# Linear attention and MLP on one NeuronCore: another start-up for batch 0 (one load for its last v, kv copied out by one engine, fill matmuls that begin later) and another tie rule in the planner

## The chip, the cores and the metric

The kernel runs on one NeuronCore of a Trainium2 chip. The metric is the device time of one execution in microseconds (us), the median of three runs. The profile is of one further execution. Short names of the engines: PE is TensorE (PEld its weight loads), DVE is VectorE, ACT is ScalarE, POOL is GpSimd, SP is SyncE.

## The reference

The inputs are q, k and v, each 8 batches x 8 heads x 576 rows x 64, in float32.

```python
kv  = einsum('bhsd,bhse->bhde', k, v)           # 64 x 64 per head, over all 576 rows
o   = einsum('bhsd,bhde->bhse', q, kv)
x   = o / sqrt(mean(o*o, -1) + 1e-6) * g_norm   # then the heads side by side: (8, 576, 512)
xn  = (x - mean(x)) / sqrt(var(x) + 1e-6) * g_ln
out = x + relu(xn @ w_ch1) @ w_ch2              # 512 -> 2048 -> 512
```

## The kernel before

**Tiles.** The 8 x 576 rows of x make 36 tiles of 128 rows: four tiles per batch ("slots" 0 to 3) and one tile for the last 64 rows of two batches together (slot 4). Tiles 0 to 3 are batch 0, tiles 4 to 7 batch 1, tile 8 their slot 4, then batch 2, and so on. Four tiles make a block.

**Per batch.** POOL loads k, v and q by DMA with a cast to bf16. `k_permute` puts k in the order of the matmul, `kv_mm` (L446) makes kv of two heads at a time in PSUM, and `kv_out` (L459 and L461) copies its two diagonal parts, `upper` false and true, into `kv_pack`. q has to be turned to `qT`: `q_turn_pe` (L410) does it on PE with the identity, and `q_turn_out` (L390, L392) copies it out of PSUM; `q_turn_dma` (L431) does it by a DMA on SP's queue. Batch 0's slots 0 to 3 and batch 1's slots 0 and 1 are turned on PE, all else by DMA. Batch 1's q comes in one load to `qb` and is put in order by four ACT copies; batch 2's comes to the same `qb` in the same way, with two copies.

**Per tile.** `t_out` (L469) makes o; ACT squares it (L482), DVE reduces (L491) and multiplies by g_norm (L486), ACT takes the root (L495), DVE inverts and scales (L500, L517), takes the mean, and makes `xc` (L543). `xc` is turned to `xT`, on PE for tiles 0 to 11 (L550, copied out by ACT, L557), by DMA on SP's queue after that (L561). The first MLP matmul is `m1` (L600 tile by tile in blocks 0 and 1, groups of 16 matmuls with 128 moving columns; L615 in later blocks, 4 matmuls of 512), with relu on ACT (L607, L622). The second is `m2` (L634, groups of 4), and DVE adds x (L641). SP stores.

**Order.** Every piece of work is registered with `add(engine, occupation, duration, key, dependencies, function)`. `run_plan` is a list scheduler that runs while the program is built: it takes at each step the instruction that could start earliest by its own cost figures, with the lower key first where several are ready, and the program is written in the order of the planned starts. So each engine has a fixed order of instructions, and the cost figures in `add` do nothing on the chip but set this order. Main MLP groups follow one list with a window of `LOOK = 8`.

**The start.** POOL issues batch 0's k in two halves of the heads, v in a half (heads 0 to 3) and two quarters (heads 4, 5 and 6, 7), q of slot 0 in two halves, then slots 1 to 3 between the four quarters of `w1`, then `w2` and batch 1. Tile 0 is worked in two halves (`HALVED`), and tiles 0 and 1 have `xc` turned in two halves (`HALF_TURN`). `idle_mm` puts fill matmuls that nobody reads into PE's stream, from 1.3 us planned time on (`WARM_FROM`), on a zeroed tile `blank`; before `kv_mm` they are as many as fit the planned gaps, later 0.6 of the gap. They come in packs of 12, 24, 13, 10 and 18. `kv_out` of batch 0 has DVE copy the lower part and ACT the upper, each waiting for `kv_mm` alone:

```python
        for u in (0, 1):
            eng, cost = (("DVE", dve_cost), ("ACT", act_cost))[u]
            ab.append(add(eng, *cost(64 * (h1 - h0) // 2), -59 + i, [s, z0], ...
```

**Later loads.** For batches from 3 on, `gate` puts a small POOL copy that reads a tile's `xT` ahead of the loads of k, q and v, so that they wait for tiles f-8, f-7 and f-6, where f is the batch's first tile (for batch 3 tiles 5, 6, 7).

Of the kernel before, what the change touches and what calls it, by code (L numbers as in the profile page):

```python
# [14 lines left out]
def kernel(  # L15
# [11 lines left out]
    nc = tc.nc  # L27
# [21 lines left out]
    XB = 18  # L49
    NEAR = 0.35  # L50
    BANKS = {"mm": 4, "out": 2, "kvt": 2}
    WARM_FROM = 1.3
    HALVED = (0,)
    SPLIT_STORE = (25,)
    HALF_TURN = (0, 1)
    PARTS = ((0, 4), (4, 8))

# [47 lines left out]
    def run_plan():  # L107
        free = dict.fromkeys(("PE", "ACT", "DVE", "POOL", "SP"), 0.0)
        free["POOL"], free["SP"], free["DVE"], free["ACT"] = 1.2, 0.7, 0.8, 2.1
        lanes = {"POOL": [], "SP": []}  # L110
        server = 3.7
        left = {e: [s for s in steps if s.eng == e] for e in free}
        mains = [s for s in steps if s.main]
        order = []

        def ready(s):
            r = 0.0
            if s.behind and s.behind.start is None:
                return None
            for d in s.deps:  # L120
                if d.done is None:
                    return None
                r = max(r, d.done + (s.lag if d.dma else 0.0))
            if s.dma and len(lanes[s.eng]) >= 8:
                r = max(r, lanes[s.eng][-8].done)
            if s.alloc and len(slots[s.alloc]) >= BANKS[s.alloc]:
                f = slots[s.alloc][-BANKS[s.alloc]].frees
                if f.done is None:
                    return None
                r = max(r, f.done)  # L130
            return r + 0.06

        while any(left.values()):
            window = set()
            for s in mains[:LOOK]:
                if (s.key < 16) != (mains[0].key < 16) or 16 <= mains[0].key < 32 and window:
                    break
                window.add(id(s))
            best = None
            for e, ls in left.items():  # L140
                cand = []
                for s in ls:
                    if s.main and id(s) not in window:
                        continue
                    r = ready(s)
                    if r is not None:
                        cand.append((max(r, free[e]), s.key, s))
                    if e == "POOL":
                        break
                if not cand:  # L150
                    continue
                t = min(c[0] for c in cand)
                near = [c for c in cand if c[0] <= t + 1e-6]
                c = min(near, key=lambda c: c[1])
                while e in ("DVE", "ACT", "PE"):

                    near = [d for d in cand if d[0] <= t + NEAR and d[1] < c[1] - 0.7
                            and c[0] + c[2].occ > d[0] + 0.1 and (e != "PE" or d[1] < -3)]
                    if not near:
                        break  # L160
                    c = min(near, key=lambda d: d[:2])
                t, s = c[0], c[2]
                if best is None or t < best[0]:
                    best = (t, s)
            assert best is not None, "the plan is stuck"
            t, s = best
            s.start = t
            free[s.eng] = t + s.occ
            if s.dma:
                lanes[s.eng].append(s)  # L170
                lat, wk, tail = s.dma
                begin = max(server, t + s.occ + lat)
                server = begin + wk
                s.done = begin + wk + tail
            else:
                s.done = t + s.dur
            if s.alloc:
                slots[s.alloc].append(s)
            left[s.eng].remove(s)
            if s.main:  # L180
                mains.remove(s)
            order.append(s)
        order.sort(key=lambda s: s.start)
        return order
# [14 lines left out]
        return s  # L199


    blank = consts.tile([128, 128], bf16, name="blank")
    nc.vector.memset(blank, 0.0)
    eps_attn = consts.tile([128, 1], f32, name="eps_attn")
    nc.vector.memset(eps_attn, EPS_ATTN)
    eps_ln = consts.tile([128, 1], f32, name="eps_ln")
# [80 lines left out]
    for i, (k_, n, c) in enumerate(groups):  # L287
# [17 lines left out]
    rate6, rate4, rate1 = 400.0, 395.0, 305.0  # L305

    load = {}
    row = [add("SP", 0.4, 1.4, -99, [], lambda x=x, f=f: nc.sync.dma_start(
        scales[:, f], bass.AP(tensor=x.tensor, offset=x.offset,
                              ap=[[x.shape[0], 1], list(x.ap[0])])))  # L310
        for x, f in ((moe_g_ln, slice(0, Dm)), (g_norm, slice(Dm, Dm + D)))]
# [48 lines left out]
    pool_load(("v", 0, 0), load_kv(vb, v, 0, 0, 4), rate6)  # L360
    pool_load(("k", 0, 4), load_kv(kb, k, 0, 4, 8), rate6)
    pool_load(("q", 0, 0, 0), load_slot(qp[0], q, 0, 0, 0, 4), rate1)
    pool_load(("v", 0, 4), load_kv(vb, v, 0, 4, 6), rate6)
    pool_load(("v", 0, 6), load_kv(vb, v, 0, 6, 8), rate6)
    pool_load(("q", 0, 0, 4), load_slot(qp[0], q, 0, 0, 4, 8), rate1)
    ident = pool_do(0.6, identity_fn)
    pool_load(("q", 0, 1), load_slot(qp[0], q, 0, 1), rate1)
# [281 lines left out]


    k0p = []
    for i, (h0, h1) in enumerate(PARTS):
        k0p.append(add("DVE", 0.13 * (h1 - h0) + 0.07, 0.13 * (h1 - h0) + 0.15, -80 + i, load["k", 0, h0],
                       lambda h0=h0, h1=h1: k_permute(nc.vector, 0, h0, h1)))
    for h0, h1 in PARTS:
        add_q_turn_pe(0, 0, load["q", 0, 0, h0], -57 + h0 / 4, ("DVE", "ACT")[h0 // 4], h0, h1)
    for t in (1, 2, 3):
        add_q_turn_pe(0, t, load["q", 0, t], (-4.5, pos[2] - 9, pos[3] - 9)[t - 1],
                      ("ACT", "ACT", "DVE")[t - 1])
    kvs = []  # L660

    urgent = []
    for i, (h0, h1) in enumerate(((0, 4), (4, 6), (6, 8))):
        hps = range(h0 // 2, h1 // 2)
        w = (h1 - h0) / 8
        s = add("PE", 1.36 * w, 1.36 * w + 0.25, -60 + i, load["v", 0, h0] + [k0p[h0 // 4]],
                lambda hps=hps, i=i: kv_mm(0, hps), alloc="kvt")
        ab = [s]
        for u in (0, 1):
            eng, cost = (("DVE", dve_cost), ("ACT", act_cost))[u]  # L670
            ab.append(add(eng, *cost(64 * (h1 - h0) // 2), -59 + i, [s, z0],
                          lambda h0=h0, h1=h1, u=u: kv_out(
                              0, h0 // 2, h1 // 2, (nc.vector, nc.scalar)[u], u == 1)))
        s.frees = ab[-1]
        kvs.append(ab[1:])
        if i == 0:
            kv_first = s
        else:
            urgent.append(s)
        kv_mm_done = s  # L680
    adone[0]["kvmm"] = kv_mm_done
    kvs[1:] = [kvs[1] + kvs[2]]
    adone[0]["kv"] = kvs[0] + kvs[1]
    load_w_kv1()
    pool_load(("q", 0, 4), load_fifth(qp[0][:, 4, :, :], q, 0), 180.0, [])
    pool_load(("q", 1, 4), load_fifth(qp[1][:, 4, :, :], q, 1), 180.0, [])
# [97 lines left out]
    def plan_tile(n):  # L784
# [8 lines left out]
            deps.append(main_at(okey[n] - EARLY))  # L793
        def cost(c, h0, h1):
            return c((h1 - h0) * D)
        halves = PARTS if n in HALVED else ((0, H),)

        q0 = okey[n] if n // 4 not in FINE else p - 12
        xs = []
        for h0, h1 in halves:  # L800
            hh = dict(h0=h0, h1=h1)
            w = (h1 - h0) / H
            q0 = p - 12 if n // 4 in FINE else okey[n]
            d = kvs[len(xs)] + [adone[0]["qT", 0][len(xs)]] if n in HALVED else deps
            o = add("PE", 0.23 * len(bs) * w, 0.23 * len(bs) * w + 0.2, okey[n], d,
                    lambda hh=hh: t_out(n, **hh), alloc="out")
            if n in HALVED:
                urgent.append(o)
            sq = add("ACT", *cost(act_cost, h0, h1), q0 + 4,
                     [o] + [done[n - 3]["red"] if n >= 3 else None], lambda hh=hh: t_sq(n, **hh))  # L810
            red = add("DVE", 0.6 * w, 0.6 * w + 0.08, q0 + 5, [sq], lambda hh=hh: t_red(n, **hh))
# [14 lines left out]
        mean = add("DVE", 0.15 if few else 0.8, 0.2 if few else 0.9, q0 + 7.5, xs, lambda: t_mean(n))  # L826
        m1_before = blk[m - 3]["m1done"] if m >= 3 else None
        turned = []
        for h0, h1 in ((0, 4), (4, 8)) if n in HALF_TURN else halves:
            ff = dict(f0=h0 * D, f1=h1 * D)  # L830
            w = (h1 - h0) / H
            xc = add("DVE", 0.6 * w + 0.06, 0.6 * w + 0.15, q0 + 8, [mean, load["gl"][0]],
                     lambda ff=ff: t_xc(n, **ff))
            if n < N_PE_TURN:
                tp = add("PE", 0.23 * w, 0.23 * w + 0.22, q0 + 8.2, [xc, ident, m1_before],
                         lambda ff=ff: t_turn_pe(n, **ff), alloc="kvt")
                if n in HALVED:
                    urgent.append(tp)
                tp.frees = add("ACT", *cost(act_cost, h0, h1), q0 + 8.5, [tp],
                               lambda ff=ff: t_turn_out(n, **ff))  # L840
                turned.append(tp.frees)
            else:
# [7 lines left out]
        if m in FINE or i == 3:  # L850
            vd = var if m in FINE else blk[m]["var"]
            e = last_pos[n if m in FINE else 4 * m] - 6
            if few:
                vd = [add("DVE", 0.33, 0.4, e, vd, lambda: b_var(n))]
            s = add("ACT", 0.2, 0.3, e + 1, vd, lambda: b_std(n))
            r = add("DVE", 0.12, 0.2, e + 2, [s], lambda: b_rstd(n))
            for j in ((n,) if m in FINE else range(4 * m, 4 * m + 4)):
# [85 lines left out]
    def idle_mm(count):  # L943
        if "idle" not in blk[0]:
            blk[0]["idle"] = psum.tile([128, 512], f32, tag="mm", name="idle_ps", bufs=BANKS["mm"])
        for _ in range(count):
            nc.tensor.matmul(blk[0]["idle"][:, 0:128], lhsT=blank, rhs=blank, start=True, stop=True)

    order = run_plan()
    first_mm = min(s.start for s in order if s.main)  # L950
    pe_end, idle = WARM_FROM, {}
    for s in order:
        if s.eng != "PE":
            continue
        if s.start <= first_mm:
            gap = s.start - pe_end
            if s.start <= kv_first.start:
                idle[id(s)] = int(gap / 0.107 + 0.5)
            elif gap > 0.3 and not s.main and (s not in urgent or gap > 1.2):
                idle[id(s)] = int(0.6 * gap / 0.056)  # L960
        pe_end = s.start + s.occ
    for s in order:
        if id(s) in idle:
# [31 lines left out]
```

## Time and profile before

| | |
|---|---|
| median of 3 runs | 294.14 us (294.11 to 294.18) |
| profiled execution, its own time | 294.14 us |
| its span in the profile | 292.4 us |
| PE busy | 284.2 us, 97% of the span |
| DVE, ACT, POOL busy | 164.4, 143.4, 65.9 us |
| granted PE clock, all 40 slices | 9 (90% of full speed or more) |
| DMA | 35.73 MB; 188 to 205 GB/s from 5 to 60 us |
| first row of m1 matmuls (L600) | 16.52 us |
| start of the last PE stretch, L634 x96 | 275.02 us |

The span is counted from the first to the last profiled instruction; the execution's own time holds 1.74 us beside it. In a row of the timeline, equal instructions in a row are merged: "4.71 2.74 PE ... x24" is 24 instructions from 4.71 us on, of which the last ended 2.74 us later. A matmul ends about 0.2 us after it was issued, while the next is already running, so the rate is read from the starts.

### The profile page before, as it was taken

How to read it: one execution, taken by the hardware profiler on the slowest of the kernel's cores; microseconds unless marked ns; L12 is line 12 of the kernel's file. 1: busy time of each engine (PE TensorE's matmuls, PEld its weight loads, DVE VectorE, ACT ScalarE, POOL GpSimd, SP SyncE). 2: the span in 40 equal slices, each digit the busy share in tenths (PEclk: the TensorE clock that was granted, in tenths of full speed). 3: DMA queues.
4: the chain of work that ended last, by engine and by line, in shares of the span. 5: the costliest groups of instructions: out<-in, count | busy, mean ns of one | idle time of the engine just before them, and what ended most of it. 6: DMA issues, size and time to landing. Idle time of an engine off the chain costs nothing.

```text
span 292.4 us, 5167 instructions
## 1 busy us (share of the span) xinstructions
PE 284.2 (97%) x2049; PEld 161.3 (55%) x2049; DVE 164.4 (56%) x357; ACT 143.4 (49%) x292; POOL 65.9 (23%) x93
## 2 busy tenths in 40 slices
PE   8869999999999999999999999999999999999995
PEld 6759945976745445444544445444544444444444
DVE  1597048468883997557655775477557755320022
ACT  3469954887846612761276127611761177017400
POOL 8983320105506405404050406000000000000000
PEclk9999999999999999999999999999999999999999
DMA  7999999943998997993999399932101310120012
GB/s 96 186 199 205 204 198 178 252 73 70 173 171 136 158 183 161 174 203 77 188 103 161 98 181 119 168 81 91 56 18 54 92 54 18 57 86 22 0 74 72
DMA packets 109116, 35.73 MB, mean 122 GB/s; under 512 B 87715, under 2 KB 104739, under 8 KB 109092
## 3 DMA queue, kind: packets, MB, share of 16 engines
q0 software_dynamic: 72624, 18.35, 64.8%
q1 hardware_dynamic: 36228, 16.92, 25.2%
q8 instruction: 16, 0.26, 0.4%
q10 hardware_dynamic: 240, 0.13, 0.2%
q14 instruction: 8, 0.07, 0.1%
HBM read 36.70 MB, written 9.44 MB: 158 GB/s over the span
## 4 chain that ended last, share of the span: by engine, by line
PE 83%; DMA 9%; POOL 6%; issue 0%; ACT 0%; DVE 0%; POOLq 0%
PE mm_ps L634 41%; PE mm_ps L615 33%; DMA qb<-in_q_dram 7%; PE mm_ps L600 4%; PE out_ps L469 3%; PE kv_ps L446 2%; DMA qT<-qp 2%; POOL qp L262 1%; POOL w L342 1%; POOL vb L241 1%; POOL kb L241 1%; PE xT_ps L550 1%; POOL w L344 0%; ACT qp L390 0%; PE qT_ps L410 0%
## 5 line engine op out<-in xcount | busy, mean ns | idle before, releaser
L634 PE MATMUL mm_ps<-w,m 128*128 128x512 bf16 (+2 forms) x608 | 129.5, 368 | 0.0
L615 PE MATMUL mm_ps<-xT,w 128*128 128x512 bf16 x448 | 100.6, 379 | 0.0
L622 ACT ACTIVATE m<-mm_ps 128x512 bf16<-128x512 f32 x112 | 66.8, 597 | 50.3 <-PE mm_ps L615 49.4
L634 PEld LDWEIGHTS <-m 128*128 128x128 bf16 x608 | 57.2, 98 | 60.8
L615 PEld LDWEIGHTS <-w 128*128 128x128 bf16 x448 | 43.1, 98 | 48.8
L491 DVE TENSOR_REDUCE ss<-sq 128x8 f32<-128x512 f32 (+1 forms) x37 | 24.8, 669 | 49.3 <-ACT sq L482 49.3
L641 DVE SCALAR_TENSOR_TENSOR x<-mm_ps,rstd,x 128x512 f32<-128x512 f32 (+2 forms) x38 | 27.3, 720 | 41.8 <-PE mm_ps L634 41.7
L482 ACT ACTIVATE sq<-out_ps 128x512 f32<-128x512 f32 (+1 forms) x37 | 21.6, 583 | 38.4 <-PE out_ps L469 38.3
L600 PE MATMUL mm_ps<-xT,w 128*128 128x128 bf16 x512 | 31.0, 219 | 1.2 <-DMA w<-in_moe_w_ch_dram 0.7
L600 PEld LDWEIGHTS <-w 128*128 128x128 bf16 x512 | 29.3, 98 | 2.5 <-issue 0.9
L543 DVE SCALAR_TENSOR_TENSOR xc<-x,mv,gl 128x512 bf16<-128x512 f32 (+1 forms) x38 | 27.2, 724 | 1.2
L486 DVE TENSOR_TENSOR xg<-out_ps,gn 128x512 f32<-128x512 f32 (+1 forms) x37 | 24.7, 668 | 0.2
L607 ACT ACTIVATE m<-mm_ps 128x512 bf16<-128x512 f32 x32 | 18.5, 597 | 3.2 <-PE mm_ps L600 2.9
L721 POOL COPY mark<-xT 128x1 bf16<-128x1 bf16 x15 | 6.3, 422 | 54.5 <-DMA xT<-xc 52.1
L495 ACT ACTIVATE rms<-ss,eps_attn 128x8 f32<-128x8 f32 (+1 forms) x37 | 11.1, 299 | 12.3 <-DVE ss L491 12.2
L521 DVE TENSOR_TENSOR x<-xg,inv 128x512 f32<-128x512 f32 x24 | 16.6, 691 | 0.8
L537 DVE BATCH_NORM_STATS2 stats<-x 128x6 f32<-128x512 f32 x24 | 16.6, 690 | 0.5
L469 PE MATMUL out_ps<-kv_pack,qT 128*128 128x128 bf16 x160 | 14.5, 219 | 1.3 <-ACT qT L390 0.7
L469 PEld LDWEIGHTS <-qT 128*128 128x128 bf16 x160 | 11.3, 98 | 8.1 <-ACT qT L390 1.1
L446 PEld LDWEIGHTS <-kp 128*128 128x128 bf16 (+1 forms) x168 | 10.6, 101 | 1.9 <-issue 0.3
L446 PE MATMUL kv_ps<-vb,kp 128*128 128x128 bf16 (+1 forms) x144 | 11.3, 226 | 0.2
L557 ACT COPY xT<-xT_ps 128x512 bf16<-128x512 bf16 (+1 forms) x14 | 7.3, 522 | 8.1 <-PE xT_ps L550 8.1
(63 smaller groups left out, 175.2 us busy)
## 6 DMA issues: line engine op xcount, KB each, us to landing
out_dram<-x SPq DMA_DIRECT2D x31, 256.0 KB, 2.3
w<-in_moe_w_ch_dram POOLq DMA_DIRECT2D x8, 512.0 KB, 12.0
vb<-in_v_dram POOLq DMA_DIRECT2D x6, 512.0 KB, 10.9
kp<-in_k_dram POOLq DMA_DIRECT2D x5, 512.0 KB, 8.5
qp<-in_q_dram POOLq DMA_DIRECT2D x5, 512.0 KB, 9.6
qb<-in_q_dram POOLq DMA_DIRECT2D x2, 512.0 KB, 19.1
out_dram<-x SPq DMA_DIRECT2D x8, 128.0 KB, 2.7
qp<-in_q_dram POOLq DMA_DIRECT2D x10, 64.0 KB, 8.7
```

What stands on the lines that cost most here:

```text
L446: nc.tensor.matmul(ps[:, hp, :], lhsT=kp[b % 2][p, t, 2 * hp:2 * hp + 2, :].rearrange("p h d -> p (h d)"), rhs=(v5[b % 2][:, 2 * hp:2 * hp ...
L469: nc.tensor.matmul(o3[:, hp, :], lhsT=att[b]["qT"][:, 4 * t + hp, :], rhs=kv_pack[b % 3][:, hp, :], start=(i == 0), stop=(i == len(bs) - 1))
L482: nc.scalar.activation(sq[:, h0:h1, :], st[n]["ps", h0][:, h0:h1, :], func=AF.Square)
L486: nc.vector.tensor_mul(xg[:, h0:h1, :], st[n]["ps", h0][:, h0:h1, :], gn.to_broadcast([128, h1 - h0, D]))
L491: nc.vector.tensor_reduce(ss[:, h0:h1, :], st[n]["sq"][:, h0:h1, :], axis=AX.X, op=ALU.add)
L543: nc.vector.scalar_tensor_tensor(xc[:, f0:f1], in0=st[n]["x"][:, f0:f1], scalar=blk[m]["mv"][:, i, 0:1], in1=gl[:, f0:f1], op0=ALU.subtrac ...
L600: nc.tensor.matmul(ps[:, d, :], lhsT=w1[c][:, kk, d * 128:(d + 1) * 128], rhs=blk[m]["xT"][:, kk, i * 128:(i + 1) * 128], start=(kk == 0), ...
L607: nc.scalar.activation(st[n]["m1"][:, c, :, :], st[n]["m1ps", c], func=AF.Relu)
L615: nc.tensor.matmul(ps, lhsT=w1[c][:, kk, d * 128:(d + 1) * 128], rhs=blk[m]["xT"][:, kk, :], start=(kk == 0), stop=(kk == nKm - 1))
L622: nc.scalar.activation(blk[m]["m1", c][:, d, :], blk[m]["m1ps", g], func=AF.Relu)
L634: nc.tensor.matmul(st[n]["m2ps", f0], lhsT=m1_piece(n, c, d), rhs=w2[c][:, d, f0:f1], start=(c == 0 and d == 0), stop=(c == 3 and d == 3))
L641: nc.vector.scalar_tensor_tensor(x[:, f0:f1], in0=st[n]["m2ps", f0], scalar=blk[m]["rstd"][:, i, :], in1=x[:, f0:f1], op0=ALU.mult, op1=AL ...
```

## The change

- v of batch 0, heads 4 to 7: one load in place of two; its `kv_mm` is one step of 12 matmuls in place of two of 6.
- `kv_out` of batch 0: both parts on DVE, one after the other.
- `blank` and the fill matmuls from 1.3 us on go. Fill matmuls read `identity` and stand in the last 9 us of planned time before the first m1 group, with 0.8 of the planned gap. They come in packs of 9, 6, 2, 6, 17, 20, 3 and 10.
- `HALF_TURN` goes: tile 1's `xc` and `xT` are made in one piece. Slot 2's q is copied out by DVE, not ACT.
- The scheduler: only DVE and ACT may take a step with a lower key that is up to 0.35 us later, by a simpler rule; some keys and cost figures differ, and its model of DMA starts at 0 us, not 3.7.

```diff
-    WARM_FROM = 1.3
+    WARM_FROM = 9.0
...
-    HALF_TURN = (0, 1)
-    PARTS = ((0, 4), (4, 8))
...
-        server = 3.7
+        server = 0.0
...
+                if e in ("DVE", "ACT"):
+                    k0 = min(c[1] for c in near)
+                    near += [c for c in cand if c[0] <= t + NEAR and c[1] < k0 - 0.7]
                 c = min(near, key=lambda c: c[1])
-                while e in ("DVE", "ACT", "PE"):
-
-                    near = [d for d in cand if d[0] <= t + NEAR and d[1] < c[1] - 0.7
-                            and c[0] + c[2].occ > d[0] + 0.1 and (e != "PE" or d[1] < -3)]
...
-    pool_load(("v", 0, 4), load_kv(vb, v, 0, 4, 6), rate6)
-    pool_load(("v", 0, 6), load_kv(vb, v, 0, 6, 8), rate6)
+    pool_load(("v", 0, 4), load_kv(vb, v, 0, 4, 8), rate6)
...
-    for i, (h0, h1) in enumerate(((0, 4), (4, 6), (6, 8))):
+    for i, (h0, h1) in enumerate(((0, 4), (4, 8))):
         hps = range(h0 // 2, h1 // 2)
-        w = (h1 - h0) / 8
-        s = add("PE", 1.36 * w, 1.36 * w + 0.25, -60 + i, load["v", 0, h0] + [k0p[h0 // 4]],
+        s = add("PE", 0.7, 0.95, -60 + i, load["v", 0, h0] + [k0p[i]],
                 lambda hps=hps, i=i: kv_mm(0, hps), alloc="kvt")
         ab = [s]
         for u in (0, 1):
-            eng, cost = (("DVE", dve_cost), ("ACT", act_cost))[u]
-            ab.append(add(eng, *cost(64 * (h1 - h0) // 2), -59 + i, [s, z0],
-                          lambda h0=h0, h1=h1, u=u: kv_out(
-                              0, h0 // 2, h1 // 2, (nc.vector, nc.scalar)[u], u == 1)))
+            ab.append(add("DVE", 0.22, 0.26, -59 + i, [ab[-1], z0],
+                          lambda h0=h0, h1=h1, u=u: kv_out(0, h0 // 2, h1 // 2, nc.vector, u == 1)))
...
-        for h0, h1 in ((0, 4), (4, 8)) if n in HALF_TURN else halves:
+        for h0, h1 in halves:
...
-            nc.tensor.matmul(blk[0]["idle"][:, 0:128], lhsT=blank, rhs=blank, start=True, stop=True)
+            nc.tensor.matmul(blk[0]["idle"][:, 0:128], lhsT=identity, rhs=identity, start=True, stop=True)
```

The built programs show what this does to the order. On PE, with a pair of numbers for tile and quarter of `w1`, the m1 groups of tiles 0 and 1 stand:

```
before: (0,0) (0,1) (1,0) (1,1) (0,2) (1,2) (0,3) (1,3)
after:  (0,0) (0,1) (1,0) (0,2) (1,1) (0,3) (1,2) (1,3)
```

Other shifts on PE: batch 1's `kv_mm` stands before the first m2 group, not behind it; batch 1's two q turns and first two `t_out` stand together; ahead of batch 2's first `t_out`, the turn of one tile's `xc` (four matmuls) now stands behind it. POOL has the same order but for the one load less; the gates and the DMA turns of q are the same in both programs, and on SP two of the later turns of q move ahead of one turn of an `xT`.

## The prediction

> **What bounds the kernel now.** I read the page first (PE busy 97% of the span, granted clock 9 in all 40 slices), then PE's waits, the chain, the timeline of the start and the table by stretches.
>
> PE's waits, whole:
>
> ```profile
> PE idle_ps L947 <- DVE eps_ln L207: 1.0, 1, 1.0
> PE out_ps L469 <- ACT qT L390: 0.7, 2, 0.5
> PE mm_ps L600 <- DMA w<-in_moe_w_ch_dram: 0.7, 1, 0.7
> PE xT_ps L550 <- DVE xc L543: 0.6, 1, 0.6
> PE out_ps L469 <- DMA qT<-qp: 0.6, 1, 0.6
> PE mm_ps L600 <- ACT xT L557: 0.3, 1, 0.3
> PE qT_ps L410 <- DMA qp<-in_q_dram: 0.3, 1, 0.3
> ```
>
> After the start, PE waits only for a quarter of `w1` (18.99 us), for tile 1's `xT` (20.63) and for batch 2's `qT` (69.03). From 69.03 us to the end it waits for nothing. What the change costs is what PE has left to do when the last such wait ends.
>
> The chain, where it is not PE:
>
> ```profile
> 19.23 19.13 DMA qb<-in_q_dram
> ...
> 38.38 0.63 ACT qp L390
> ...
> 62.45 6.54 DMA qT<-qp
> ...
> 69.03 0.62 PE out_ps L469 x8
> ```
>
> The marks at which PE is held are landings of DMAs. The change moves no DMA but one, so I ask at each mark how late PE may come.
>
> The timeline of the start:
>
> ```profile
> 4.71 2.74 PE L947 MATMUL idle_ps<-blank 128*128 128x128 bf16 x24
> ...
> 7.56 1.44 PE L446 MATMUL kv_ps<-vb,kp 96*128 96x128 bf16 x12
> ...
> 8.79 1.43 PE L947 MATMUL idle_ps<-blank 128*128 128x128 bf16 x13
> ...
> 12.25 0.28 PE L469 MATMUL out_ps<-kv_pack,qT 128*128 128x128 bf16 x2 [0.52 <-ACT qT L390]
> ...
> 12.59 0.72 PE L947 MATMUL idle_ps<-blank 128*128 128x128 bf16 x10
> ...
> 18.99 1.07 PE L600 MATMUL mm_ps<-xT,w 128*128 128x128 bf16 x16 [0.68 <-DMA w<-in_moe_w_ch_dram]
> ```
>
> Between starts, 128 columns take 0.107 us in the first packs and 0.056 in the pack at 12.59. The starts inside the pack at 8.79 change over at 9.9 us, so full rate came 5.2 us after the gapless stretch began at 4.71, though the granted clock reads 1.00 throughout.
>
> The table by stretches:
>
> ```profile
> 5.00:10.00 5.00, 4.89 (x49) 4.73 (x47) 1.22 (x4) 0.35 (x2) 4.92 (x8) 1.00 1.39 188
> 20.00:40.00 20.00, 19.75 (x294) 16.97 (x291) 8.53 (x29) 17.25 (x38) 6.66 (x10) 1.00 1.29 205
> ```
>
> The last column is GB/s: loads run at 188 to 205 from 5 us on, one after another.
>
> **The change part by part.**
>
> *One load less.* POOL's two quarter loads take 1.28 us (row "4.20 1.28 ... x2"); one takes about 0.64. All later issues come 0.64 us earlier, the bytes are the same. Bounds: 0, if the transfers set the landings, and -0.64 if the issues do. I take 0, for at 205 GB/s the queue has no holes for an earlier issue to fill.
>
> *kv and the fills.* Here the order of the built program is walked with durations of the trace, at the slow 0.107 us first. v's first half lands as before: 12 `kv_mm` from 7.56 to 8.84, nine fills to 9.80, two q turns, six fills to 10.65. The first `t_out` needs four DVE copies in a row (kv 0.28, k 0.54, q 0.29, kv 0.28) and stands near 10.8; two fills to 11.2; 12 `kv_mm` in place of 2 x 6, to 12.5; their two copies, 0.28 each and both now on DVE, to 13.2. PE has turns and fills until 13.57, then tile 0's second `t_out`. Before it stood at 12.25, so this is +1.3 us. From there to the `xT` turn took 3.3 us before (12.25 to 15.55), so the turn comes by 16.9, two ACT copies later m1 begins at 17.7 to 17.9 (last part before: 17.15), and ends after 16 x 0.056 = 0.9 at 18.6 to 18.8. The cover is the next group's wait for `w1`, which ended at 18.99 in a stall of 0.68. So both kernels start group (0,1) at about 19.0: cost 0, with 0.1 to 0.4 us to spare. Without that cover it would be up to 0.7.
>
> *Tile 1 turned in one piece.* Before, m1 had 2 of its 16 matmuls at 20.63 and the rest from 20.97 to 21.75. Now: group (0,1) to 19.9, q and `xT` turns to 20.3; ACT has the relu of (0,1) until 20.66, then the copy of 512 columns (0.58) to 21.25; 16 matmuls to 22.19. Behind by 0.44.
>
> *Another order of m1.* Group (0,3) now has one group less ahead of it, and it needs the last quarter of `w1`. That lands, after the first one PE waited for (18.95), when 128 KB of q and two quarters of 512 KB are through: 1.18 MB at 205 GB/s is 5.75 us, so 24.7; I use 24.8. PE comes to it at 22.2 + 0.22 (`t_out`) + 2 x 0.89 + 0.22 = 24.4 and waits 0.4. Before, (0,3) began at 24.87 with one more group (0.89) done. So PE is behind by 0.89 - 0.06 = 0.83, however good the start is, and has 0.4 to spare if the start is worse.
>
> *Batch 1's q.* From there PE is dense. Before, it stood 0.24 us at 39.06 (12 matmuls of 0.216 from 36.23 end at 38.82). A later PE finds the q copied (38.38 + 0.63), so 0.83 - 0.24 = +0.6 is left. The second turned q needs ACT's four copies (38.38 + 2.18) and one of 0.59, at 41.15; its `t_out` comes at 41.2. Cost 0 to 0.1: the one place where a cover is that thin.
>
> *The wait at 69.03.* Before, PE could have issued the `t_out` at 68.04 + 0.22 = 68.26. Now it comes 0.6 later, but four transposes (0.22) stand behind it in place of ahead: 68.64. The DMA turn of q went out at 62.45, after ACT's two copies (60.43, 1.99 us), before which ACT stood idle 0.60 us for the load; ACT's relus are 0.6 later now, so that wait is just closed. The landing stays, and PE still waits 0.39.
>
> *After it.* The same work plus the 0.22 us. On SP two q turns (3.1 to 5.0 us each to issue) move ahead of an `xT` turn. The nearest row: an `xT` turn behind such a q turn goes out at 161.84, and its block's m1 begins at 173.42, so some 10 us cover it; without them it would be up to 5.
>
> **Sum.** Late at the last `w1`: 0.83. At 69.03: 0.83 - 0.24 - 0.22 = 0.37, less than the 0.77 by which PE was early there, so nothing of it is left. Behind it: +0.22 us. The profiled execution took 294.14 us, its span 292.4 and 1.74 around it, and the median of the runs is the same 294.14. So 292.6 + 1.74 = 294.4.
>
> **A rule against it.** The stretch without fills before 7.56 us delays full rate. By the row (5.2 us of gapless matmuls) it comes at 12.8, which the walk above bears: +0.22. [...]
>
> **Rivals.**
>
> *The slow rate lasts.* If it holds until the fills are through, the fills themselves block PE: from the second `t_out` (13.8 at that rate) to m1 there are 50 fills and 12 other matmuls, 62 x 0.107 = 6.6 us, so m1 starts at 20.4 and group (0,1) at 21.5, 2.5 late. Of that, 2.1 beyond the 0.44; the spare 0.4 at `w1` and 0.39 at `qT` absorb 0.8. Result +0.22 + 1.3, up to +1.8 if the first group is slow too: 295.7 to 295.9. It decides from about 17 us on, each fill after that costing 0.05. For it: full rate took 5.2 us of fills before, and 8.9 counted from the first pack at 1.0. Against: from 7.56 on PE's new stream has hardly a hole.
>
> *The landings move.* If issues set them, every mark comes 0.64 earlier; PE's own start is then late by 0.64 - 0.4 more and the gain is about 0.4: 293.7. Against: 188 GB/s already at 5 to 10 us.
>
> *A cover fails.* If the landing of `qT` slips with PE (ACT's copies or the stores ahead on the same DMAs), nothing of the 0.6 is absorbed: +0.6 to +0.83, 294.7 to 295.0.
>
> *It does not do what it says.* The turns of q by DMA and the gates of later loads are the same in both programs, so nothing comes from them.
>
> **Chances.** The forecast has 0.70, its own range 294.0 to 294.7 (0.3 for durations and thin covers). The slow rate has 0.17, with 294.8 to 295.9 by its length; the failing cover 0.08; landings that move 0.05. A measurement of this kernel can tell about 0.2%, 0.59 us, from no change: the bounds are 293.55 and 294.73. Faster is left with 0.04, slower gets most of the slow rate and of the failing cover, 0.22, no change 0.74. The range 293.7 to 295.6 leaves out the longest slow rate and what no case names.
>
> **What would show it.** After: 0.056 us between starts by about 13 us; group (0,1) at 19.0; a wait for `w1` near 24.8 that was not there; no wait near 39; one for `qT` at 69.03, 0.2 to 0.4 us; no PE wait later; PE's last stretch from 275.24. The forecast is wrong if slow starts are seen after 17 us, if 69.03 moves, or if PE waits anywhere after 70 us.

## The result and the profile after

The changed kernel takes 295.38 us, the median of six runs (294.52 to 295.93), and the kernel before 294.16 us in six runs beside it (293.88 to 294.54). The ratio of the means is 1.0038, with a 95% interval of 1.0022 to 1.0054: slower by more than the 0.2% that the prediction calls measurable, where it gave 0.74 to no change. It is 1.0 us above the forecast of 294.4, outside the 294.0 to 294.7 of that case and inside the wide range of 293.7 to 295.6. The profiled execution took 295.59 us, with a span of 293.8 (292.4 before).

PE's waits of the changed kernel, whole:

```profile
PE kv_ps L437 <- DMA vb<-in_v_dram: 3.9, 1, 3.9
PE scale_ps L308 <- DMA scales<-in_moe_g_ln_dram: 2.3, 1, 2.3
PE mm_ps L591 <- ACT xT L548: 0.7, 1, 0.7
PE out_ps L460 <- DMA qT<-qp: 0.5, 1, 0.5
```

The wait for `w1` at 18.99 us and the short one at 39.06 are gone, because PE comes later to both. The wait for batch 2's `qT` is still there. The timeline of PE at the marks that the prediction names:

```profile
8.55 1.44 PE L437 MATMUL kv_ps<-vb,kp 96*128 96x128 bf16 x12 [3.90 <-DMA vb<-in_v_dram]
...
14.20 0.27 PE L460 MATMUL out_ps<-kv_pack,qT 128*128 128x128 bf16 x2
...
19.41 1.06 PE L591 MATMUL mm_ps<-xT,w 128*128 128x128 bf16 x16
...
21.83 1.05 PE L591 MATMUL mm_ps<-xT,w 128*128 128x128 bf16 x16 [0.67 <-ACT xT L548]
...
25.06 2.13 PE L591 MATMUL mm_ps<-xT,w 128*128 128x128 bf16 x35
```

At 25.06 stands the first group on the last quarter of `w1`, which landed at 25.01. And the chain:

```profile
19.33 19.19 DMA qb<-in_q_dram
...
41.61 19.59 DMA qb<-in_q_dram
61.19 0.02 issue
...
63.23 6.50 DMA qT<-qp
69.73 0.05 issue
69.78 0.62 PE out_ps L460 x8
```

Here is the first place where the forecast breaks. Batch 2's q was issued 0.18 us later than before (41.61 against 41.43) and landed 0.78 later (61.19 against 60.41); its turn was issued 0.78 later, and PE's mark moved from 69.03 to 69.78. What stands behind the mark took what was predicted: PE's last matmul ends at 288.92 before and 289.89 after, 219.89 and 220.11 us behind the mark. So +0.97 us at PE's end is +0.75 at the mark and +0.22 behind it. The other 0.45 of the span's 1.4 lies behind PE's end: 3.45 us before, 3.90 after.

**Where q lost its 0.8 us.** At 44.5 us the loads were 0.24 late, at 49.3 (batch 2's k) 1.3 us. The DMA view from 45 to 48 us, after (40 slices of 0.075 us: busy share of the 16 DMA engines in tenths, then what they moved), and one of its queues:

```profile
DMA  9999999999999999999999101110499999999999
GB/s 198 191 184 183 172 406 157 171 157 160 159 162 155 159 167 130 114 101 75 49 31 14 10 10 10 10 10 10 43 142 155 167 174 169 169 171 167 174 166 155
...
q8 instruction: 1, 0.02, 2.0%
```

The same view of the kernel before:

```profile
DMA  9999999999999999999999999999999999999999
GB/s 177 188 171 177 174 183 196 177 189 149 157 184 167 172 174 193 169 177 167 157 177 162 166 154 177 162 152 159 152 140 140 121 154 108 162 155 161 160 155 166
```

After, nearly nothing moves for some 0.5 us, with a decline of 0.4 us ahead of it. Of the data packets in the trace, 28 of that time took over 0.5 us, up to 1.08; before, none did between 38 and 70 us. What stands just in front of the hole is one packet of 16 KB on queue 8, from 45.40 us on, 0.95 us long. The page of the changed kernel lists the queues (packets, MB, share of 16 engines):

```profile
q0 software_dynamic: 72608, 18.35, 64.4%
q1 hardware_dynamic: 36228, 16.92, 25.5%
q8 instruction: 16, 0.26, 0.4%
```

Queue 8 has the same row on the page of before. I take its 16 packets for PE's program, fetched while it runs: when each went out, PE and PEld had begun the same number of rows in both traces to within 26, at times up to 3.7 us apart (137.67 and 141.37). After, the 4,117 rows of PE and PEld in the trace (4,090 of them matmuls and weight loads) are 257 for each packet, or 128 pairs of weight load and matmul. The one in front of the hole is the fourth; before, the fourth came at 43.87, and the DMA turns of q began to move data at 44.84.

The next but one of these packets falls into the turn of batch 2's q in both kernels, at 66.96 and 67.66. The DMA view from 62.4 to 70.4 us (0.2 us a slice), before:

```profile
GB/s 0 0 0 0 0 0 118 221 212 207 214 209 212 230 214 210 225 210 210 225 202 273 396 328 358 113 0 10 10 10 20 20 10 0 0 0 0 0 0 0
```

In the trace each load or turn lands in 16 parts. Of this turn 15 had landed by 67.42, and the 16th came at 68.98 (after: 68.14 and 69.73); the 10 GB/s at the end are what was left of it. So the mark at 69.03, which the prediction took for a landing of data and nothing else, had 1.56 us of something else in it. Without them the turn would have been whole ahead of the 68.26 at which PE could have come: the 0.77 us of slack that the prediction counted on there came from this late part.

### The profile page after: what moved, and what is told of

It is laid out like the page before. It is cut to its first block, busy times and chain, and to the rows that moved or that the text cites. A ratio compares the mean times of both kernels' runs of the same rounds, so it can differ in the third digit from the quotient of the medians.

```text
span 293.8 us, 5156 instructions
## 1 busy us (share of the span) xinstructions
PE 282.3 (96%) x2045; PEld 160.3 (55%) x2045; DVE 164.9 (56%) x357; ACT 142.6 (49%) x287; POOL 66.0 (22%) x92
## 4 chain that ended last, share of the span: by engine, by line
PE 75%; DMA 18%; POOL 3%; ACT 1%; issue 1%; DVE 0%; POOLq 0%
PE mm_ps L625 36%; PE mm_ps L606 33%; DMA qb<-in_q_dram 13%; DMA kb<-in_k_dram 2%; PE out_ps L460 2%; DMA qT<-qp 2%; PE kv_ps L437 2%; PE mm_ps L591 1%; ACT qp L381 1%; POOL kb L233 1%; POOL w L334 1%; POOL w L336 0%; POOL vb L233 0%; PE xT_ps L541 0%; POOL qp L254 0%
## 5 line engine op out<-in xcount | busy, mean ns | idle before, releaser
L702 POOL COPY mark<-xT 128x1 bf16<-128x1 bf16 x15 | 6.9, 458 | 56.0 <-DMA xT<-xc 53.5
L452 DVE CAST kv_pack<-kv_ps 64x256 bf16<-64x256 f32 (+1 forms) x18 | 7.1, 393 | 16.4 <-PE kv_ps L437 16.1
```

## The experiments

Theory **"instruction loads"**: PE's position in its own program decides when queue 8's packets go out; one that meets a DMA turn of q can stall all 16 engines for about 1 us, or hold one of them up. What the change does to the time is mostly that it moves such a packet from 43.87 to 45.4. Rivals: the stall is **chance**; **the program's order or issues move the loads**; **PE's lateness** passes through to the end. All 13 traces beside the kernel before, in one table (from the packets and landings of each trace; "queue 8": the fourth and the sixth of its 16 packets; "hole": start of a group of 20 and more data packets over 0.5 us before 70 us; "PE": start of batch 2's first `t_out`; the last column is PE's end less that):

| kernel | median us | queue 8, the two packets | hole | q lands | qT: 15th, 16th part | PE | to PE's end |
|---|---|---|---|---|---|---|---|
| before | 294.16 | 43.87, 66.96 | none | 60.41 | 67.42, 68.98 | 69.03 | 219.89 |
| before again | 294.06 | 43.75, 66.59 | none | 60.09 | 67.09, 68.66 | 68.70 | 219.89 |
| 15 matmuls more, late | 294.13 | 42.84, 64.83 | 65.0 | 59.94 | 68.22, 68.23 | 68.97 | 219.87 |
| 40 matmuls more, late | 295.72 | 41.62, 63.30 | none | 60.39 | 69.26, 69.26 | 70.94 | 219.87 |
| 10 fills fewer | 295.08 | 45.70, 67.96 | 46.7 | 61.46 | 68.44, 69.98 | 70.03 | 219.89 |
| no early fills | 294.05 | 49.80, 67.22 | 50.6 | 60.92 | 67.79, 67.80 | 68.61 | 219.88 |
| 36 fills more | 293.84 | 38.39, 61.17 | none | 59.78 | 66.76, 66.77 | 68.45 | 219.88 |
| before, planner's rule of after | 294.62 | 44.17, 65.29 | 65.5 | 60.45 | 68.35, 68.36 | 68.88 | 220.10 |
| before, v and kv_out of after | 294.98 | 45.19, 67.34 | 45.7 | 60.97 | 67.84, 69.41 | 69.45 | 220.11 |
| after | 295.38 | 45.40, 67.66 | 46.1 | 61.19 | 68.14, 69.73 | 69.78 | 220.11 |
| after again | 295.27 | 46.14, 68.61 | 46.5 | 61.98 | 69.06, 70.64 | 70.68 | 220.11 |
| after, 40 early fills | 294.16 | 38.99, 61.45 | none | 59.89 | 66.75, 66.80 | 68.57 | 220.10 |
| after, 10 early fills | 294.70 | 45.80, 68.17 | 46.8 | 61.66 | 68.66, 70.24 | 70.29 | 220.11 |
| after, kv_out by two engines | 295.53 | 46.07, 67.67 | 46.4 | 61.04 | 68.09, 69.67 | 69.72 | 220.11 |

The fourth packet keeps to PE's place in its program and not to the time: when it went out, PE and PEld had begun 961 to 988 of their recorded rows in all 14 traces, at times from 38.39 to 49.80 us. Whether a hole follows goes, in these traces, by what moves meanwhile. The turns' 256-byte packets begin to move between 44.61 and 45.95 us. In the seven traces with a hole between 45 and 51 us the fourth packet was still on its way then or came later; in the other seven it had ended by then, to within 0.01 us (with the planner's rule alone 44.17 + 0.94 us, against 45.10). In the kernel before it had ended 0.08 us ahead.

An instruction packet is not the only thing that such a hole follows. At 85.42 us, where PE waits for nothing, 20 data packets took up to 1.95 us in the kernel before, and no packet of an instruction queue stood between 79.6 and 92.3 us (DMA view, 84 to 88 us, 0.1 us a slice):

```profile
GB/s 219 224 307 262 259 279 320 275 190 240 268 284 253 295 253 236 136 133 138 105 79 28 44 38 36 21 22 4 10 10 10 10 18 102 212 289 289 292 292 289
```

Nor does each packet that meets a turn make one: at 161.80 us in the same trace 289 of a turn's packets moved around it, and none took over 0.05 us. What else it takes was not tested.

**The two kernels again, unaltered.** No edit.

> The changed kernel, unaltered, for a second trace. In its first trace batch 2's q landed at 61.19 us (before 60.41), its qT at 69.73 (68.98), PE's first matmul on it stood at 69.78 (69.03), the last PE stretch at 275.99 (275.02), and the last stores took 0.4 us longer. At 46.1 us every DMA engine had packets of up to 1.08 us. Theory 'chance': that stall is no part of the program; the second trace has none there, q lands near 60.4, the qT mark is back at 69.0 to 69.2, the last stretch at 275.2 to 275.4, and the time is 294.4 to 294.8. Theory 'the program moves the loads': the stall, or another loss of the same size, is there again, the mark is at 69.6 to 69.9, the time 295.2 to 295.6.

> The kernel before, unaltered, for a second trace. Theory 'chance': stalls of the DMA engines fall in other places than in the first trace, and where one falls before 60 us the qT mark moves from 69.03 by about its length. Theory 'the program moves the loads': the mark stays within 0.2 us of 69.03. Time 294.1 by both.

Measured: 295.27 us, ratio 1.0036 [1.0022, 1.0049], and 294.06, 1.0 [0.9991, 1.0009]. The second trace of the changed kernel has the stall again, 33 packets of up to 1.44 us from 46.49 on, right behind queue 8's packet at 46.14; the second trace of the kernel before has none there. So, with the table, the stall is not chance. Neither theory had the size right for the marks: they lie 0.9 us (after) and 0.3 us (before) from those of the first traces, so a mark of one trace is good to several tenths only.

**Does PE's lateness reach the end?** The kernel before, with matmuls that nobody reads in front of group (1,3):

```diff
+        for _ in range(15 if (n, c) == (1, 3) else 0):      # 40 in the second kernel
+            nc.tensor.matmul(ps[:, 0, :], lhsT=blank, rhs=blank, start=True, stop=True)
         for d in range(4):
```

> The kernel before with 15 matmuls of 128 columns that nobody reads, put at the head of the last m1 group of tile 1 (1,3), behind PE's last wait for w1: PE is 15 x 0.056 = 0.84 us later there, as much as the change makes it by my walk, and the start is as before. Theory 'waits absorb': 0.24 goes at the wait of 39.06, the other 0.6 at the wait for batch 2's qT (0.77 early before), the mark stays at 69.0, the end at 294.1 to 294.3. Theory 'lateness passes through' (the landing of qT slips with PE): 294.7 to 295.0.

> The same with 40 such matmuls: 2.24 us late. Theory 'waits absorb': 0.24 at 39.06 and 0.77 at the qT mark go, so 1.23 us is left: 295.4. Theory 'lateness passes through': 2.0 to 2.24 us, 296.1 to 296.4. If the qT mark is itself later by part of the 2.24, the difference of the two says how much of PE's lateness the loads take on.

Measured: 294.13 us, 0.9999 [0.9990, 1.0009], and 295.72, 1.0052 [1.0039, 1.0065]. PE at batch 2's q, with 15:

```profile
68.97 0.61 PE L469 MATMUL out_ps<-kv_pack,qT 128*128 128x128 bf16 x8
```

The turn itself had met its packet near its start, at 64.83, stood still for 1.2 us (DMA view, 62.4 to 70.4 us, 0.2 us a slice) and then landed whole, at 68.23:

```profile
GB/s 0 0 0 0 0 0 136 219 211 211 193 214 298 148 10 0 3 8 10 9 42 288 289 291 292 289 362 430 389 328 0 0 0 0 0 0 0 0 0 0
```

No wait stands on PE's line: 0.84 us of lateness has used up the slack of the kernel before and no more, and the time is the same. But the extra matmuls moved the packets too: here the late part is gone, and it is the stall in the turn that put the landing at 68.23. With 40 the mark is at 70.94 and the time 1.6 us longer, 0.3 more than the theory; in that trace v's first half also landed at 8.78 us, and PE was late at the start. So that 0.84 us of late PE did not reach the end, the core of the prediction, is shown; of the 2.24 us some 0.6 did not.

**Fewer and more PE instructions.** The changed kernel with 40 fills ahead of the first kv (and a zeroed `blank`), and the kernel before with 10 of its 24 taken away:

```diff
+    early = [12, 28]
     for s in order:
+        if s.eng == "PE" and early and (len(early) == 2 or s is kvs_first):
+            idle_mm(early.pop(0), blank)
```

```diff
-                idle[id(s)] = int(gap / 0.107 + 0.5)
+                idle[id(s)] = int(gap / 0.107 + 0.5) - (10 if s is kv_first else 0)
```

> The changed kernel with 40 more fill matmuls on a zeroed tile ahead of batch 0's first kv (12 ahead of the scales' matmuls, 28 behind them), where PE stands idle 3.9 us for v; nothing else differs, so PE's 16 KB instruction loads (queue 8, one every 128 pairs of weight load and matmul) come 80 instructions sooner. Theory 'instruction loads': in both traces of the changed kernel one stands at 45.40 or 46.14 us, while DMA turns of q are moving, and packets of all 16 DMA engines then took over 1 us; and one stands at 67.66 or 68.61 us in the turn of batch 2's q, whose 16th part lands 1.6 us behind the 15th. Moved to about 40.5 and 62.5 us, both go: q lands near 60.4, all 16 parts of qT together by 67.6, PE no longer waits there, and the time is 294.2 to 294.5. Theory 'the program moves the loads' (issues, stores): the mark stays at 69.6 or later and the time at 295.0 to 295.4. Theory 'the early fills matter for the clock': full rate from about 9 us on, the first m1 group earlier, and the mark unchanged.

> The kernel before with 14 fills in place of 24 ahead of batch 0's first kv: PE's instruction loads come 20 instructions later, at about 45.5 and 67.6 us where they stood at 43.87 and 66.96, the places they have in the changed kernel; the loads of v, kv_out and the order of the work are as before. Theory 'instruction loads': all 16 DMA engines stall near 46 us for about 1 us, q lands at 61.0 to 61.3 (60.41), the mark goes to 69.6 to 69.9, and the time to 294.7 to 295.0. Theory 'the changed order moves the loads': the mark stays at 69.0 and the time at 294.1.

Measured: the changed kernel becomes 294.16 us, 1.0 [0.9991, 1.0009]: all of its loss is gone. The kernel before becomes 295.08, 1.0025 [1.0014, 1.0037], with ten matmuls that nobody reads taken out and nothing put in. The turn of batch 2's q in the changed kernel with 40 fills (62.4 to 70.4 us) ends at once on all engines, and PE does not wait for it:

```profile
GB/s 0 0 0 45 210 220 215 198 216 223 211 221 218 219 215 220 219 214 190 23 0 287 379 420 226 0 0 0 0 0 0 0 0 0 0 0 0 0 6 40
```

```profile
68.57 0.61 PE L462 MATMUL out_ps<-kv_pack,qT 128*128 128x128 bf16 x8
```

And the kernel before with 10 fills fewer has the hole (46.0 to 48.4 us, 0.06 us a slice) and the late mark:

```profile
GB/s 145 160 166 130 154 158 154 137 147 134 139 137 81 58 49 58 53 45 38 30 32 19 21 15 6 13 6 13 6 13 9 11 9 94 152 201 169 166 186 188
```

```profile
70.03 0.62 PE L469 MATMUL out_ps<-kv_pack,qT 128*128 128x128 bf16 x8 [0.71 <-DMA qT<-qp]
```

These two decide against the program's order and issues: 80 instructions more in the one kernel, 20 fewer in the other, in a place where PE stands idle, move the packet, the stall and the time, with loads, issues and order as they were. With the 40 fills the start was also earlier (m1 at 17.17, against 18.26), so that run does not exclude the start alone. In the kernel with 10 fewer m1 began at 16.58, against 16.52, and group (0,1), behind `w1`, at 19.31, against 18.99, less than the 0.84 us that cost nothing above.

**No early fills at all.**

```diff
-                idle[id(s)] = int(gap / 0.107 + 0.5)
+                idle[id(s)] = 0
```

> The kernel before without the 36 fills ahead of batch 0's first kv: the start loses what the change takes from it in fills, alone, and PE's instruction loads come 72 instructions later. Theory 'waits absorb': full rate comes at 12 to 13 us as in the changed kernel, hidden by the wait for w1 at 18.99: 0. Theory 'instruction loads': the load of 43.87 goes to about 50 us, among the turns of q (q may land up to 0.8 later, at 61.2, hidden), the load of 66.96 to about 70.5, behind the turn of batch 2's q, whose parts land together; PE then comes to it at 68.3 in place of 69.03 and the time is 293.4 to 293.6. Rival, the slow rate: m1 starts 0.6 us or more later and 0.4 or more of it stays: 294.5 and above.

Measured: 294.05 us, 0.9999 [0.9985, 1.0014]. The slow-rate rival falls: without the 36 fills ahead of the first kv the time is the same. With 36, 26 and no fills there the kernel before takes 294.16, 295.08 and 294.05 us, so the loss with 26 does not come of having fewer fills. The stall came as expected (50.6 us, q at 60.92), but the packet that follows two later went to 67.22 and not to 70.5, inside the turn, and yet all parts landed together (67.79 and 67.80). So a packet inside a turn does not always hold its 16th part up; here it was the next turn whose 16th part came late, at 70.53 against 68.72 for the 15th. The 0.5 us gain that was expected from PE's coming at 68.3 did not show: PE came at 68.61.

**kv copied out by two engines, in the changed kernel.**

```diff
-            ab.append(add("DVE", 0.22, 0.26, -59 + i, [ab[-1], z0],
-                          lambda ...: kv_out(0, h0 // 2, h1 // 2, nc.vector, u == 1)))
+            eng, cost = (("DVE", dve_cost), ("ACT", act_cost))[u]
+            ab.append(add(eng, *cost(64 * (h1 - h0) // 2), -59 + i, [ab[-1], z0],
+                          lambda ...: kv_out(0, h0 // 2, h1 // 2, (nc.vector, nc.scalar)[u], u == 1)))
```

> The changed kernel with the upper part of batch 0's kv copied by ACT, the lower by DVE (still one after the other); the planner then places some fills and turns differently, with 4 more pairs on PE. Theory 'kv_out on one engine costs': the second t_out comes 0.2 to 0.3 us earlier and 0.2 to 0.3 us of the time goes with it. Theory 'waits absorb': nothing of it is left at the qT mark, and the time follows the instruction loads: 295.2 where one stands at 44.5 to 48 us and one at 66 to 68, less where not. A 16th 8 KB instruction load at 290.5 us stood in both traces of the changed kernel among the last stores, which took 0.4 us longer than before; with other counts on ACT and DVE it may go, and 0.4 us with it.

Measured: 295.53 us, 1.0037 [1.0025, 1.005]. The second `t_out` came at 14.14 (14.20), and stall, late 16th part and mark are as in the changed kernel. So taking kv_out off the one engine does not bring the time back; as the copies still stand one after the other, the second `t_out` came hardly earlier. On the last stores: here no 8 KB packet stands at 290 us, and 3.44 us lie between PE's end and the span's; but the repeat of the changed kernel and the one with 40 fills have such a packet (291.37, 289.28) and 3.46. So the 0.45 us of the first trace is not explained by that packet alone, and stays open as one trace's.

**The parts of the change alone.** The kernel before with the planner's rule of after, and the kernel before with one load for v's last half and kv copied out by DVE:

```diff
-                while e in ("DVE", "ACT", "PE"):
...
+                if e in ("DVE", "ACT"):
+                    k0 = min(c[1] for c in near)
+                    near += [c for c in cand if c[0] <= t + NEAR and c[1] < k0 - 0.7]
```

```diff
-    pool_load(("v", 0, 4), load_kv(vb, v, 0, 4, 6), rate6)
-    pool_load(("v", 0, 6), load_kv(vb, v, 0, 6, 8), rate6)
+    pool_load(("v", 0, 4), load_kv(vb, v, 0, 4, 8), rate6)
...
+            ab.append(add("DVE", *dve_cost(64 * (h1 - h0) // 2), -59 + i, [ab[-1], z0], ...
```

> The kernel before with the changed kernel's tie rule in the planner alone: v in three loads, kv copied out by two engines, the early fills and the tile turned in halves stay. On PE the m1 groups of tiles 0 and 1 then stand in the changed kernel's order, and there are 8 fills more. Theory 'the order': PE is 0.4 to 0.8 us later behind w1, as in the changed kernel, and the time 295.0 to 295.4. Theory 'instruction loads': 16 instructions sooner and PE 0.4 to 0.8 later leaves the load of 43.87 at 43 to 44 us, ahead of the turns' data; no stall near 46, q at 60.4, the mark at 68.7 to 69.2, and the time 294.1 to 294.4.

> The kernel before with the two stated parts alone: batch 0's last v in one load, and kv copied out by DVE alone, both parts one after the other. The planner moves some fills (PE has 3 pairs more). My walk: the second t_out 0.8 to 1.3 us later than 12.25, the w1 landings within 0.2 us of before, m1's first group at 17.7 or earlier, all of it hidden by the wait for w1 at 19.0: 294.1 to 294.4, if the instruction loads stay near 43.5 and 66.7. A rival: what the start loses shows at the end, 294.5 to 295.0.

Measured: 294.62 us, 1.0010 [0.9998, 1.0022], and 294.98, 1.0031 [1.0019, 1.0043]. With the rule alone the packet stands at 44.17, ahead of the turns' data at 45.10, and there is no hole near 46; the later one, at 65.29, stalls batch 2's turn instead (65.5), all parts land at 68.36, and PE comes at 68.88 by itself. Between both expectations, with an interval that includes no change. With v and kv_out alone the expectation of 294.1 to 294.4 is missed, on the condition that it named: the packet went to 45.19, and hole, q and 16th part followed. The start shows it was not PE's lateness: group (0,1) began 0.2 us earlier than before.

```profile
18.76 1.07 PE L599 MATMUL mm_ps<-xT,w 128*128 128x128 bf16 x16 [0.58 <-DMA w<-in_moe_w_ch_dram]
...
69.45 0.62 PE L468 MATMUL out_ps<-kv_pack,qT 128*128 128x128 bf16 x8 [0.91 <-DMA qT<-qp]
```

So these two parts alone bring most of the loss (0.83 us of 1.22), and by this trace not through a later start. The other parts (tile 1 in one piece, the fills' new places, the planner's other figures) were not run alone.

**Both packets out of the way in the kernel before.** 36 fills more, in gaps of PE:

```diff
+        for _ in range(12 if (n, c) == (0, 1) else 0):
+            nc.tensor.matmul(ps[:, 0, :], lhsT=blank, rhs=blank, start=True, stop=True)
...
+        if (n, h0) in ((0, 4), (1, 0)):
+            idle_mm({0: 9, 1: 4}[n])
...
+        if n == 0 and f0 == 0:
+            idle_mm(11)
```

> The kernel before with 36 fills more, put where PE stands idle anyway: 9 ahead of tile 0's second t_out (0.74 us between starts there), 4 ahead of tile 1's (0.41), 11 ahead of tile 0's turn of xc (0.86), 12 in front of group (0,1), which waits for w1 (0.90); at 0.056 us each. PE's instruction loads then come 72 instructions sooner. Theory 'instruction loads': the loads of 43.87 and 66.96 go to about 39 and 62 us, all 16 parts of batch 2's qT land together by 67.4, PE comes at 68.3 to 68.6 and does not wait; at 68.3 the end is 0.7 us earlier: 293.4 to 293.7, a version ahead of both. Theory 'the mark is set by the loads of k, v and q alone': 69.0, and 294.1. If the fills do not fit, the start is later and uses up the gain: 294.1 and above.

Measured: 293.84 us (293.38 to 295.9), 0.9994 [0.998, 1.0008]. The packets went to 38.39 and 61.17, q's turn was whole at 66.77, and PE came to it at 68.45 without a wait. The median lies 0.3 us below the kernel before beside it (294.15), the lowest of all here, but the interval includes no change: the 293.4 to 293.7 that was expected, a version ahead of both, is not shown.

**A small shift in the changed kernel.** As with the 40 fills, with `early = [0, 10]`.

> The changed kernel with 10 fills (20 PE instructions) ahead of batch 0's first kv, where PE stands idle: a small shift of the instruction loads, the mirror of the kernel before with 10 fewer. Theory 'instruction loads': the load of 45.40 goes to 43.6 to 44.4, ahead of the turns' data as in the kernel before, so no stall near 46 and q lands at 60.0 to 60.5; the next load still falls into the turn of batch 2's q, whose 16th part is late, so the mark is at 68.7 to 69.1; from the mark to PE's end there are 220.1 us, as in all kernels with the changed order, and the time is 294.2 to 294.5: the case that the prediction had worked out. Theory 'the 40 fills of the other run helped by the clock, not by the instruction loads': 10 fills change little, the stall and the mark at 69.7 to 70.7 stay, 295.2 to 295.6.

Measured: 294.70 us, 1.0014 [1.0005, 1.0023], between the two expectations: about half of the loss is gone. The trace does not show the case that was meant. Its execution is the slowest of the eleven (295.67; the others 294.32 to 295.11), and in it `w1` came late:

```profile
20.23 1.07 PE L593 MATMUL mm_ps<-xT,w 128*128 128x128 bf16 x16 [1.11 <-DMA w<-in_moe_w_ch_dram]
...
70.29 0.62 PE L462 MATMUL out_ps<-kv_pack,qT 128*128 128x128 bf16 x8 [0.21 <-DMA qT<-qp]
```

`w1`'s second quarter landed at 20.18 us, not at 19.04 (15 of its 16 parts by 18.64); PE was that much later at 45 us, and the packet went to 45.80 in spite of 20 instructions more. That a late PE takes the packet with it fits the theory; that the ten other executions had no stall is not shown, for there is no trace of them.

## Why the prediction was right or wrong, point by point

- *The time.* That 295.38 lies in the stated range is luck. Its upper part stood there for the slow rate, which was refuted, and the case that the sum worked out ended at 294.7.
- *One load less: 0.* Right in the sum, but not all issues came 0.64 us earlier. `w1`'s first two quarters were issued 0.76 us earlier and landed 0.4 and 0.1 us later, so these issues don't set the landings. Then POOL stood 0.58 us for a landing of k, and the third quarter went out at 11.33, against 11.31 before.
- *The start.* The second `t_out` came at 14.20, not 13.57, and m1 began at 18.26, not at 17.7 to 17.9, as v's first half landed at 8.51, not 7.52 (15 of its 16 parts by 7.08). Group (0,1) came at 19.41: the cover of 19.0 was exceeded by 0.4. Full rate (0.056 us between starts, 0.107 just before) came between 13.13 and 13.19 us, 4.6 us after the almost gapless stretch began at 8.55; the walk had 12.8, an estimate from the 5.2 us of before.
- *Tile 1 in one piece, and the order of m1.* The order came as drawn, but tile 1's group began at 21.83, with a wait of 0.67 us for `xT`, and not at 21.25. PE was at the group on the last quarter of `w1` by 24.95, and `w1` landed at 25.01: of the wait of 0.4 that was to hide the rest 0.1 was left, and the 0.83 became about 1.1.
- *Batch 1's q: absorbs 0.24.* Right; no wait stands near 39 us, and the thin cover at 41.2 held.
- *The wait at 69.03.* The step that failed is its last sentence, "The landing stays, and PE still waits 0.39." PE did wait (0.46); but the landing moved by 0.75. PE was later than the 68.64 of the sum: by the starts it could have come at 69.15 (68.29 + 4 x 0.216), of which 0.27 was a stop at 64.72, behind ACT's copies of the late q. So with the old landing its lateness would have been hidden but for 0.1 at most. I had taken the landing as a matter of the q loads, their issue and ACT's copies. The runs show a second thing in it: PE's own instruction loads, which PE's lateness and the number of its instructions move (the fourth packet stood at 38.39 to 49.80 us in the 14 traces); q landed 0.78 later behind the hole, and both marks held a 16th part about 1.6 us behind the 15th. The page of before showed them, "q8 instruction: 16", and I read past that row.
- *After it: +0.22.* Right to 0.01: 219.87 to 219.89 us from the mark to PE's end in all seven traces with the four transposes ahead of `t_out`, 220.10 to 220.11 in all seven with them behind.
- *The rivals.* "A cover fails" came nearest: the landing slipped as it said, by neither of the two causes that it named, and at +0.75 + 0.22, above its 0.6 to 0.83. It had 0.08. The slow rate was refuted by the changed kernel's trace (0.056 us between starts from 13.19 us on) and by the kernel without early fills.
- *Around the span.* The last stores' 0.45 us in one trace was in no step; it is not part of what the medians show for certain.

What stays open: whether a 16 KB packet holds one engine so that the turn's other 15 wait for it in step (that fits a hole of about the packet's own 0.95 us, but was not isolated), why holes also come without such a packet (85.42 us), and what of the spread between runs comes from v's and `w1`'s landings at the start, where single parts came up to 1.5 us late too: v's at 8.51 us in the changed kernel, ahead of the first packet of queue 8 (19.12).

## What to carry to other kernels

Before a landing is used as a fixed mark, look at when its 16 parts land and what else moved then, instruction loads included: a mark with one late part (here 1.54 to 1.59 us behind the 15th in eight traces) is not a property of the data. A wait absorbs a late engine only if what ends the wait does not depend on that engine, and in this kernel the fetched program was such a dependence: with its fourth packet at 43.87 us PE's mark stood at 69.03, with it at 45.40 at 69.78. Where a small change costs more than its parts explain, put harmless instructions into an idle place and see whether the time moves.

## What the runs showed of the hardware

- Queue 8, which the page lists as instruction, moved 16 packets of 16 KB while the kernel ran, 0.88 to 1.65 us each in the traces of before and after, counted by the page on the same 16 DMA engines as the data (0.4% of their span). That they are PE's program is read from where PE stands when they go out: the fourth went out with 961 to 988 rows of PE and PEld begun in all 14 traces, and 16 packets for 4,117 rows are 257 rows each.
- In the nine traces with a hole before 70 us, such a packet began 0.2 to 1.0 us ahead of it and DMA turns were moving data; 20 to 33 data packets took over 0.5 us then, the longest of each trace 0.8 to 1.6 us. The packets on queue 8 between 15 and 35 us (before at 16.62, 25.94 and 32.79, after at 19.12, 26.95 and 34.48), where no turn was moving, were followed by no data packet over 0.5 us before the turns began (44.84 and 44.95). A hole of the same kind at 85.42 us in the kernel before had no such packet near it.
- In eight traces, with a packet late in batch 2's turn, the turn had its 16th part 1.54 to 1.59 us behind the 15th.
- Taking ten matmuls that nobody reads out of an idle stretch made the kernel before 0.25% slower (295.08 us).
